# Attention and two gated MLPs on one core: transposed scores of chunks 0 and 1 as 2 x 288 and 2 x 224 columns over two PSUM banks

## The chip, the core and the metric

The program runs on one core of one Trainium2 chip. Its metric is the device time in microseconds, from start to end of one execution; the time of a kernel is the median of several. One execution of the kernel before was also taken by the hardware profiler, which records when each instruction of each engine starts. TensorE is PE in the rows, its weight loads are PEld, VectorE is DVE, ScalarE is ACT, GpSimd is POOL, and SyncE's queue of DMA issues is SPq.

## What is computed

Attention over 4 batches and 8 heads (32 heads in all), 576 positions, head dimension 64, and then two gated MLPs over the 2304 tokens. The attention has a causal mask and a bias that comes from a running sum of `s`:

```python
scores = scale * np.matmul(q, k.transpose(0, 1, 3, 2))
s_pos = np.maximum(s, 0.0)
cum = np.cumsum(s_pos, axis=-1)
bias = -(cum[:, :, :, None] - cum[:, :, None, :])
scores = np.where(causal, -1000000000.0, scores + np.minimum(bias, 0.0))
attn = softmax(scores)                     # exp of scores minus row maximum, over its sum + 1e-9
x = np.matmul(attn, v)                     # heads side by side: 2304 x 512
x = (1 / (1 + np.exp(-(x @ w_gate))) * (x @ w_val)) @ w_out
out = ((x @ w_a) * (x @ w_b)) @ w_out2
```

## The kernel before

**Two parts.** `attention()` runs first, then `mlps()`. Both are written as lists of operations with an engine, dependencies and a priority; `Schedule.emit` puts them in order while the program is built. For attention it is called with `in_order=True` (L718): of the operations that are ready it always takes the one with the smallest priority, and the durations written beside them play no part. The order on each engine is then fixed, and semaphores hold the engines to the data.

**One head.** The 576 keys are cut into five chunks: four of 128 and a tail of 64. `head(i)` (L519) first computes scores with queries on the partitions, for the row maximum (`scores`, L551, into `ps_g`, or `ps_x` for a few; `maxima`, L566, on DVE; a transpose `mT`, L577, into `ps_t`; a copy `mc` on ACT and a DMA `md` that puts the maxima into an extra row of the query operand). Then it computes the scores a second time, transposed, with keys on the partitions: `scores_t(c)` (L588) for each chunk c, over the queries from 128 c to 575 only, since earlier queries may not see these keys. Each such product has a high and a low part, which add up in PSUM: L594 writes, L595 adds.

**Where the transposed scores lie.** The kernel's PSUM tiles have 512 or 1024 fp32 columns, one or two banks, and none of its products crosses from one bank to the next. Chunks 0 and 1 share `ps_e` of two banks (1024 columns): chunk 0, with 576 columns, lies at columns 0 to 575 and is cut at 512, so that one product has 512 columns and one has 64; chunk 1, with 448 columns, lies at 576 to 1023 in one piece. Chunks 2 and 3 (320 and 192 columns) share `ps_f`, and chunk 4 (64) uses `ps_t`. ACT takes the exponential of each of the three tiles in one instruction (`expo`, L597, operations `ex`) and writes it to `pt` in SBUF, with the same order of columns; `P0` (L354) names where each chunk begins in `pt`. POOL then clears the masked half of the diagonal blocks of 128 x 128 (`causal`, L610, operations `cs`): the first two blocks by one instruction, as a list of two blocks at a fixed distance.

**Two heads.** `pair(j)` (L625) takes two heads together. `values` (L635) multiplies `pt` by the values `vx`; the heads lie side by side on PSUM partitions 0 to 63 and 64 to 127 of `ps_x`. It runs once over queries 128 to 575 and once over queries 0 to 127. `sums_of` (L645) multiplies `pt` by ones for the denominators, in five rounds over two thirds of the queries each. These products read `pt` as fp32; the trace records two matmuls for each of them.

**Around it.** In the same loop SP loads q, k and v, POOL and DVE make the low parts (L536, L538), and the first weights of the MLP are loaded and split. DVE, ACT and POOL all take turns between heads. `mlps()` then runs matmuls of 384 and 512 columns on PE (L290 to L292) to the end.

The change touches `P0`, `head` (`cols`, `scores_t`, `expo`, the loop over `ex`, `causal`) and `pair` (`cols_of`, `values`, `sums_of`).

Of the kernel before, what the change touches and what calls it, by code (L numbers as in the profile page):

```python
# [11 lines left out]
ACTF = mybir.ActivationFunctionType  # L12
# [14 lines left out]
class Schedule:  # L27
# [9 lines left out]
    def op(self, name, eng, dur, fn, deps, prio, acq=None, rel=None, lat=None):  # L37
        rel = () if rel is None else rel if isinstance(rel[0], tuple) else (rel,)
        self.ops[name] = (eng, dur, fn, deps, prio, acq, rel, self.LAT if lat is None else lat)
# [80 lines left out]
def attn_mlp_kernel(  # L120
# [14 lines left out]
    nc = tc.nc  # L135


    B, H, S = s.shape
    D = vt.shape[-1]
# [4 lines left out]
    TL = S - 4 * 128  # L144
    rows = [128] * 4 + [TL]
# [9 lines left out]
    scale = 1.0 / float(D) ** 0.5  # L155
# [20 lines left out]
    if wide:  # L176
        u = const.tile([128, 512], I32, name="u")
# [155 lines left out]
    def attention():  # L333
        with ExitStack() as c2:
# [16 lines left out]
            KB = R1 + 2  # L351
            NO, NR2, NX, NPT = 4, 4, 4, 4
            QD, QV = 384, 128
            P0 = [0, 576, 1024, 1344, 1536]  # L354
            CQ1, CK1 = 0, 640
            xt = [tile2([128, S], FP32, f"xt{i}") for i in range(NX)]
            rb = tile2([128, S], FP32, "rb")
# [3 lines left out]
            ones = tile1([128, 32], FP32, "ones")  # L361
# [36 lines left out]
            def more():  # L398
# [4 lines left out]
                for t in pt_t:  # L403
                    nc.vector.memset(t[TL:128, P0[4]:], 0.0)

# [28 lines left out]
            def selectors(o):  # L434
# [3 lines left out]
            sc = Schedule({  # L438
                "g": [psum1("ps_g", 1024)],
                "E": [psum1("ps_e", 1024)],  # L440
                "F": [psum1("ps_f")],
                "t": [psum1("ps_t")],
                "px": [psum1("ps_x", 1024)],
                "raw": list(raw_t),
                "u": [0],
                "W": wslot[:2],
                "stg": stg,
            })
            op = sc.op
# [49 lines left out]
            for i in range(3):  # L499
                op(("relk", i), "SP", 0.65, lambda i=i: nc.sync.dma_start(  # L500
                    out=f32(o_t[i][D:R1, CK1:CK1 + S]), in_=f32(rel[i:NR * BH:BH])), ["sums"] + [("ms", i)] * (i > 0), -210 + i, lat=2.2)
# [17 lines left out]
            def head(i):  # L519
                b, h = divmod(i, H)  # L520
                t0 = HT * i
                o, o2, r, pt = o_t[i % NO], p_t[i % 3], r_t[i % NR2], pt_t[i % NPT]
# [6 lines left out]
                if i >= 3:  # L529
# [7 lines left out]
                    out=k2[up], in0=r[dn], in1=f32(k2[dn]), op=ALU.subtract), [("hk2", i)], (-8.7, -8.3)[i] if i < 2 else t0 - HT - 0.3)  # L537
                op(("loq", i), "DVE" if i < 2 else "Pool", 0.9 if i < 2 else 1.4, lambda: (nc.vector if i < 2 else nc.gpsimd).tensor_tensor(  # L538
                    out=q2[dn], in0=r[up], in1=f32(q1[up]), op=ALU.subtract), [("hq1", i)] + done2, -151 + 2 * i if i < 2 else t0 - HT + 1.45)
# [8 lines left out]
                for g, cs in ((0, (3, 2, 0)), (1, (1, 4))):  # L548
                    to = ("px", ("S", i)) if g and first_at else ("g", (i, g))
# [32 lines left out]
                    out=f32(o[KB:KB + 1, CQ1:CQ1 + 640]), in_=f32(mr)), [("mc", i)] + done, (-8.7, -8.4)[i] + 0.06 if i < 2 else t0 - HT + (3.93, 5.21)[i % 2], lat=2.2)  # L582


                tiles = {0: ("E", (i, 0)), 1: ("E", (i, 0)), 2: ("F", (i, 0)), 3: ("F", (i, 0)), 4: ("t", ("p", i))}
                cols = {0: 0, 1: 576, 2: 0, 3: 320, 4: 0}

                def scores_t(c):  # L588
                    ps = sc.get(*tiles[c])
                    n, c0, q0 = rows[c], cols[c], 128 * c  # L590
                    ks = slice(q0, q0 + n)
                    for a, e in ([(0, 512), (512, 576)] if c == 0 else [(q0, S)]):
                        to = ps[0:n, c0 + a - q0:c0 + e - q0]
                        nc.tensor.matmul(out=to, lhsT=k1[:, ks], rhs=q1[:, a:e], start=True, stop=False)  # L594
                        nc.tensor.matmul(out=to, lhsT=k2[:, ks], rhs=q2[:, a:e], start=False, stop=True)  # L595

                def expo(c0, c1, src):  # L597
                    n = rows[c0]
                    a, e = P0[c0], P0[c1] + S - 128 * c1
                    nc.scalar.activation(  # L600
                        out=pt[0:n, a:e], in_=sc.get(*src)[0:n, cols[c0]:cols[c0] + e - a], func=ACTF.Exp, scale=scale)

                for c in range(NC):
                    op(("ST", i, c), "PE", (0.69, 0.41, 0.3, 0.23, 0.23)[c], lambda c=c: scores_t(c),
                       [("md", i), ("lok", i), ("loq", i)], t0 + (4.2, 4.8, 5.2, 5.5, 5.8)[c], acq=tiles[c] if c in (0, 2, 4) else None)
                for e, (c0, c1, d) in enumerate(((0, 1, 1.05), (2, 3, 0.62), (4, 4, 0.25))):
                    op(("ex", i, e), "ACT", d, lambda c0=c0, c1=c1: expo(c0, c1, tiles[c0]),
                       [("ST", i, c0), ("ST", i, c1), ("pd", (i - NPT) // 2)], t0 + (5.4, HT + 0.3, HT + 0.9)[e], rel=tiles[c0])

                def causal(e):  # L610

                    n, a, st_ = ((128, P0[0], P0[1] - P0[0]), (128, P0[2], P0[3] - P0[2]), (TL, P0[4], 0))[e]
                    w = 2 if st_ else 1
                    to = pt[0:n, a:a + n] if w == 1 else bass.AP(
                        tensor=pt.tensor, offset=pt[0:n, a:a + 1].offset, ap=[list(pt.ap[0]), [st_, 2], [1, n]])
                    nc.gpsimd.affine_select(to, to, [[0, 2], [1, n]][2 - w:], ALU.is_ge, 0.0, base=0, channel_multiplier=-1)
# [8 lines left out]
            def pair(j):  # L625

                t0, b, h = HT * 2 * j, 2 * j // H, 2 * j % H
                vx, x, t = vx_t[j % 2], xt[j % NX], sc_t[j % 2]
                pts = [pt_t[(2 * j + e) % NPT] for e in range(2)]
                pxk = ("px", j) if j < NH // 2 - 1 else ("g", ("pv", j))  # L630

                def cols_of(c, a):
                    return P0[c] + a - 128 * c

                def values(q0, q1_):  # L635
                    px = sc.get(*pxk)
                    js = [c for c in range(NC) if 128 * c < q1_]
                    for c in js:
                        a = max(q0, 128 * c)
                        for e in range(2):  # L640
                            nc.tensor.matmul(  # L641
                                out=px[e * D:(e + 1) * D, QD + a:QD + q1_], lhsT=vx[:, e, c], rhs=pts[e][:, cols_of(c, a):cols_of(c, q1_)],
                                start=c == 0, stop=c == js[-1], skip_group_check=True)

                def sums_of():  # L645

                    px = sc.get(*pxk)
                    rounds = [((0, 0, 192), (0, 384, 576)), ((0, 192, 384), (1, 384, 576)), ((1, 128, 320), (2, 384, 576)),
                              ((2, 256, 384), (3, 384, 576)), ((1, 320, 384), (4, 512, 576))]
                    for n, steps in enumerate(rounds):  # L650
                        for u, (c, a, z) in enumerate(steps):
                            for e in range(2):
                                p = 64 * e + 32 * u
                                nc.tensor.matmul(  # L654
                                    out=px[p:p + 32, a - QD * u:z - QD * u], lhsT=ones, rhs=pts[e][:, cols_of(c, a):cols_of(c, z)],
                                    start=n == 0, stop=n == len(rounds) - 1, skip_group_check=True)

                op(("lv", j), "SP", 1.2, lambda: load_v(j), [("pv", j - 2, 0), ("sel", 1)], t0 + 4.6, lat=3.0)
                op(("pv", j, 1), "PE", 2.6, lambda: values(QV, S), [("cs", 2 * j + e, c) for e in range(2) for c in range(3)] + [("lv", j)], t0 + 3 * HT + 1.3, acq=pxk)
# [34 lines left out]
            for e, (ld, ab, *dv) in enumerate(LOADS):  # L694
                n, m = e // 2, e % 2
                prio = HT * ld + (0.5 if e > 2 else 0)
                last = convert(sc, n, m, [("S", max(int(ld) - 1, 0), 0)], prio,
                               at=[HT * ab + 1.2 - prio] + [HT * dv[k] + 0.95 + y - prio for k, y in ((0, 0), (0, 0.01), (1, 0), (2, 0))])
# [311 lines left out]
```

## Time and profile before

| | |
|---|---|
| median of three runs | 1028.08 us (1027.7 to 1032.49) |
| the profiled execution | 1028.64 us |
| its span, first to last instruction | 1026.9 us |
| mean granted TensorE clock | 0.997 |
| PE busy, share of the span | 98% |
| first matmul of the MLP part | 199.35 us |

Two views count most. The timeline lists instructions in order of time; since matmuls overlap in the records, the cost of one is read from its start to the start of the next, not from its length. The chain of waits follows back from the last instruction what each step waited for; where it names PE, a shorter product can end the program earlier.

### The profile page before, as it was taken

Reading aid. Unit: us, or ns where it says so; the run is one execution under the profiler, and the core shown is the slowest. Engines: PE = TensorE matmul, PEld = TensorE weight load, DVE = VectorE, ACT = ScalarE, POOL = GpSimd, SP = SyncE. Lnnn points to the kernel's source line nnn. Section 1 sums busy time; section 2 is a strip of 40 time slices with the busy share of each in tenths; the row PEclk is TensorE's granted clock in tenths of the full one; section 3 lists DMA queues with packets and bytes.
Section 4 is the critical chain, followed back from the end, with each engine's and each line's share of the span. In section 5 each row is a group of like instructions: output and inputs, shape, how many; then the busy total and the mean of one; then the engine's idle time right before and its main releaser. Section 6 shows DMA issues by size and latency. Waiting matters only on the chain.

```text
span 1026.9 us, 17097 instructions
## 1 busy us (share of the span) xinstructions
PE 1007.2 (98%) x6160; PEld 911.2 (89%) x6160; DVE 691.2 (67%) x1130; ACT 466.3 (45%) x891; POOL 389.3 (38%) x388
## 2 busy tenths in 40 slices
PE   6999999999999999999999999999999999999998
PEld 5777777799999999998888899999999999888886
DVE  7887789889598665779764239867866477932222
ACT  3676767555555454463442245244333334422221
POOL 5578797641555344233200014254533432400000
PEclk8999999999999999999999999999999999999999
DMA  6668786341334223456644342133422245544433
GB/s 171 174 170 203 215 218 188 105 157 47 109 123 144 88 103 112 141 179 205 205 137 123 90 143 72 62 106 125 133 99 103 88 163 175 174 138 133 114 103 102
DMA packets 93586, 139.76 MB, mean 136 GB/s; under 512 B 16215, under 2 KB 54863, under 8 KB 93502
## 3 DMA queue, kind: packets, MB, share of 16 engines
q1 hardware_dynamic: 89234, 133.03, 41.4%
q10 hardware_dynamic: 2988, 4.95, 2.0%
q8 instruction: 48, 0.79, 0.3%
q0 software_dynamic: 1280, 0.70, 0.3%
q14 instruction: 36, 0.29, 0.1%
HBM read 85.53 MB, written 33.45 MB: 116 GB/s over the span
## 4 chain that ended last, share of the span: by engine, by line
PE 82%; DVE 7%; DMA 4%; issue 2%; ACT 1%; POOL 1%; SPq 1%; ACTq 0%; DVEq 0%; POOLq 0%
PE ps L290 24%; PE ps L291 24%; PE ps L292 24%; PE ps_x L641 2%; PE ps_g L557 2%; PE ps_x L654 1%; PE ps_e L594 1%; PE ps_e L595 1%; DVE nm L570 1%; DVE s L823 1%; DMA o<-o 1%; DVE raw L220 1%; DVE u L218 1%; DVE u L216 1%; DMA raw<-in_moe_w_val_dram 1%
## 5 line engine op out<-in xcount | busy, mean ns | idle before, releaser
L290 PE MATMUL ps<-rg,wk 128*128 128x384 f32 (+2 forms) x1128 | 382.1, 339 | 2.5 <-DVE s L823 2.4
L292 PE MATMUL ps<-rg,wk 128*128 128x384 f32 (+2 forms) x1128 | 381.3, 338 | 0.0
L290 PEld LDWEIGHTS ps<-rg,wk 128*128 128x128 f32 x1128 | 211.9, 188 | 8.8 <-DVE s L823 4.5
L292 PEld LDWEIGHTS ps<-rg,wk 128*128 128x128 f32 x1128 | 211.9, 188 | 3.7
L823 DVE TENSOR_TENSOR s<-ps,s 128x384 f32<-128x384 f32 x216 | 119.0, 553 | 114.9 <-PE ps L292 66.5
L291 PE MATMUL ps<-x_sb,wk 128*128 128x384 f32 x576 | 192.6, 334 | 0.0
L836 POOL TENSOR_TENSOR hs<-s,s 128x384 f32<-128x384 f32 x72 | 88.6, 1230 | 265.4 <-issue 93.1
L291 PE MATMUL ps<-rg,wk 128*128 128x384 f32 (+2 forms) x552 | 188.6, 342 | 0.0
L820 ACT COPY s<-ps 128x384 f32<-128x384 f32 x216 | 103.2, 479 | 182.7 <-PE ps L292 180.9
L268 POOL TENSOR_TENSOR wk<-raw,wk 128x512 fp32r<-128x512 f32 x96 | 127.5, 1355 | 147.1 <-ACT wk L265 131.8
L903 DVE TENSOR_TENSOR rg<-rg 128x512 fp32r<-128x512 f32 (+1 forms) x120 | 80.0, 671 | 111.2 <-ACT rg L902 108.4
L902 ACT CAST rg<-rg 128x512 fp32r<-128x512 f32 (+1 forms) x120 | 68.5, 578 | 147.2 <-DMA rg<-hd 109.3
L291 PEld LDWEIGHTS ps<-x_sb,wk 128*128 128x128 f32 x576 | 108.2, 188 | 0.1
L291 PEld LDWEIGHTS ps<-rg,wk 128*128 128x128 f32 x552 | 103.7, 188 | 3.7
L570 DVE TENSOR_REDUCE nm<-ps_g 128x1 f32<-128x512 f32 (+4 forms) x154 | 74.4, 532 | 25.0 <-PE ps_g L562 24.0
L292 PE MATMUL ps<-rg,rg 128*128 128x512 f32 (+1 forms) x228 | 86.2, 378 | 0.0
L290 PE MATMUL ps<-rg,rg 128*128 128x512 f32 (+1 forms) x228 | 86.2, 378 | 0.0
L291 PE MATMUL ps<-rg,rg 128*128 128x512 f32 (+1 forms) x228 | 86.2, 378 | 0.0
L215 ACT ACTIVATE mag<-raw 128x512 f32<-128x512 f32 x72 | 48.3, 671 | 57.1 <-DVE raw L223 31.1
L220 DVE SCALAR_TENSOR_TENSOR raw<-raw,u 128x512 int32<-128x512 int32 x72 | 63.4, 881 | 4.1
L831 ACT ACTIVATE s<-s 128x384 f32<-128x384 f32 x72 | 37.9, 527 | 52.0 <-DVE s L823 51.8
L218 DVE SCALAR_TENSOR_TENSOR u<-raw,u 128x512 int32<-128x512 int32 x72 | 60.4, 839 | 1.5
(119 smaller groups left out, 1495.6 us busy)
## 6 DMA issues: line engine op xcount, KB each, us to landing
hd<-hs SPq DMA_DIRECT2D x72, 384.0 KB
rg<-hd SPq DMA_DIRECT2D x72, 256.0 KB
raw<-in_moe_w_out_dram SPq DMA_DIRECT2D x24, 512.0 KB
r<-in_qk_dram SPq DMA_DIRECT2D x32, 288.0 KB
rg<-hd SPq DMA_DIRECT2D x72, 128.0 KB
raw<-in_moe_w_gate_dram SPq DMA_DIRECT2D x12, 512.0 KB
raw<-in_moe_w_val_dram SPq DMA_DIRECT2D x12, 512.0 KB
raw<-in_moe_w_a_dram SPq DMA_DIRECT2D x12, 512.0 KB
```

The lines of the kernel that those rows point to most:

```text
L218: ("DVE", 0.65, lambda: nc.vector.scalar_tensor_tensor(out=u, in0=parts(n, m)[1], scalar=-0x40000000, in1=u, op0=ALU.bitwise_and, op1=ALU. ...
L220: ("DVE", 0.65, lambda: nc.vector.scalar_tensor_tensor(out=parts(n, m)[1], in0=parts(n, m)[0], scalar=29, in1=u, op0=ALU.logical_shift_rig ...
L268: return lambda: nc.gpsimd.tensor_tensor(out=wcols(n, a, w, 1), in0=src(), in1=f32(wcols(n, a, w, 0)), op=ALU.subtract)
L290: nc.tensor.matmul(out=outp, lhsT=wh, rhs=xh, start=start and e == 0, stop=False, skip_group_check=True)
L291: nc.tensor.matmul(out=outp, lhsT=wh, rhs=xl, start=False, stop=False, skip_group_check=True)
L292: nc.tensor.matmul(out=outp, lhsT=wl, rhs=xh, start=False, stop=stop and e == n - 1, skip_group_check=True)
L570: nc.vector.tensor_reduce(out=nm[0:n, c:c + 1], in_=ps[0:n, p0:p0 + nk], axis=AX.X, op=ALU.max)
L820: op((x,) + key, "ACT", ACT_P, lambda x=x: nc.scalar.copy(out=s(x), in_=bank("X")), [P(p)], end(p) - 10, acq=("s", key + (x,)))
L823: return lambda: nc.vector.tensor_tensor(out=s(x), in0=bank(b_), in1=s(x), op=ALU.add)
L836: op(("h2",) + key, "Pool", PTT, lambda: nc.gpsimd.tensor_tensor(out=half(1), in0=s("s4"), in1=s("s2"), op=ALU.mult), [("c22",) + key, (g[ ...
L902: op(("hh",) + key, "ACT", 0.17 + 0.00083 * N, lambda hs=hs, N=N: nc.scalar.copy(out=hs()[:, 0, 0:N], in_=f32(hs()[:, 1, 0:N])), [("hl",) ...
L903: op(("ho",) + key, "DVE", 0.157 + 0.00104 * N, lambda hs=hs, N=N: nc.vector.tensor_tensor(out=hs()[:, 1, 0:N], in0=f32(hs()[:, 1, 0:N]), ...
```

## The change

The transposed scores of chunks 0 and 1 are cut and placed otherwise in `ps_e` and `pt`. Chunk 1 is cut at query 352 (`QM`) into two products of 224 columns: the first goes to columns 0 to 223, the second to 800 to 1023. Chunk 0 goes between them, at 224 to 799, as two products of 288 columns, whose border at 512 is that of the banks. There are thus eight products a head for these chunks, before six. The exponential covers the same 1024 columns. The mask's two blocks now lie 224 columns apart, before 576. The value and sums products that read chunk 1 on both sides of query 352 read a list of two pieces, and write their output as two pieces that adjoin (new helper `product`). Nothing else differs: operations, priorities, dependencies and tiles are those of before.

```diff
--- before.py
+++ after.py
@@ -351,7 +351,8 @@
             KB = R1 + 2
             NO, NR2, NX, NPT = 4, 4, 4, 4
             QD, QV = 384, 128
-            P0 = [0, 576, 1024, 1344, 1536]
+            P0 = [224, 0, 1024, 1344, 1536]
+            QM = 352
             CQ1, CK1 = 0, 640
             xt = [tile2([128, S], FP32, f"xt{i}") for i in range(NX)]
             rb = tile2([128, S], FP32, "rb")
@@ -583,33 +584,34 @@
 
 
                 tiles = {0: ("E", (i, 0)), 1: ("E", (i, 0)), 2: ("F", (i, 0)), 3: ("F", (i, 0)), 4: ("t", ("p", i))}
-                cols = {0: 0, 1: 576, 2: 0, 3: 320, 4: 0}
+                cols = {0: P0[0], 1: P0[1], 2: 0, 3: 320, 4: 0}
 
                 def scores_t(c):
                     ps = sc.get(*tiles[c])
-                    n, c0, q0 = rows[c], cols[c], 128 * c
+                    n, q0 = rows[c], 128 * c
                     ks = slice(q0, q0 + n)
-                    for a, e in ([(0, 512), (512, 576)] if c == 0 else [(q0, S)]):
-                        to = ps[0:n, c0 + a - q0:c0 + e - q0]
+                    for a, e in ([(0, 288), (288, S)] if c == 0 else [(q0, QM), (QM, S)] if c == 1 else [(q0, S)]):
+                        at = cols[c] + a - q0 + (S if c == 1 and a == QM else 0)
+                        to = ps[0:n, at:at + e - a]
                         nc.tensor.matmul(out=to, lhsT=k1[:, ks], rhs=q1[:, a:e], start=True, stop=False)
                         nc.tensor.matmul(out=to, lhsT=k2[:, ks], rhs=q2[:, a:e], start=False, stop=True)
 
-                def expo(c0, c1, src):
-                    n = rows[c0]
-                    a, e = P0[c0], P0[c1] + S - 128 * c1
+                def expo(c0, n):
+                    p = rows[c0]
+                    a, b_ = (0, 0) if c0 == 0 else (P0[c0], cols[c0])
                     nc.scalar.activation(
-                        out=pt[0:n, a:e], in_=sc.get(*src)[0:n, cols[c0]:cols[c0] + e - a], func=ACTF.Exp, scale=scale)
+                        out=pt[0:p, a:a + n], in_=sc.get(*tiles[c0])[0:p, b_:b_ + n], func=ACTF.Exp, scale=scale)
 
                 for c in range(NC):
                     op(("ST", i, c), "PE", (0.69, 0.41, 0.3, 0.23, 0.23)[c], lambda c=c: scores_t(c),
                        [("md", i), ("lok", i), ("loq", i)], t0 + (4.2, 4.8, 5.2, 5.5, 5.8)[c], acq=tiles[c] if c in (0, 2, 4) else None)
-                for e, (c0, c1, d) in enumerate(((0, 1, 1.05), (2, 3, 0.62), (4, 4, 0.25))):
-                    op(("ex", i, e), "ACT", d, lambda c0=c0, c1=c1: expo(c0, c1, tiles[c0]),
+                for e, (c0, c1, n, d) in enumerate(((0, 1, 1024, 1.05), (2, 3, 512, 0.62), (4, 4, TL, 0.25))):
+                    op(("ex", i, e), "ACT", d, lambda c0=c0, n=n: expo(c0, n),
                        [("ST", i, c0), ("ST", i, c1), ("pd", (i - NPT) // 2)], t0 + (5.4, HT + 0.3, HT + 0.9)[e], rel=tiles[c0])
 
                 def causal(e):
 
-                    n, a, st_ = ((128, P0[0], P0[1] - P0[0]), (128, P0[2], P0[3] - P0[2]), (TL, P0[4], 0))[e]
+                    n, a, st_ = ((128, P0[1], P0[0] - P0[1]), (128, P0[2], P0[3] - P0[2]), (TL, P0[4], 0))[e]
                     w = 2 if st_ else 1
                     to = pt[0:n, a:a + n] if w == 1 else bass.AP(
                         tensor=pt.tensor, offset=pt[0:n, a:a + 1].offset, ap=[list(pt.ap[0]), [st_, 2], [1, n]])
@@ -629,8 +631,13 @@
                 pts = [pt_t[(2 * j + e) % NPT] for e in range(2)]
                 pxk = ("px", j) if j < NH // 2 - 1 else ("g", ("pv", j))
 
-                def cols_of(c, a):
-                    return P0[c] + a - 128 * c
+                def product(out, lhsT, pt, c, a, z, start, stop):
+                    at = P0[c] + a - 128 * c + (S if c == 1 and a >= QM else 0)
+                    rhs = pt[:, at:at + z - a]
+                    if c == 1 and a < QM < z:
+                        rhs = bass.AP(tensor=pt.tensor, offset=pt[:, at:at + 1].offset, ap=[list(pt.ap[0]), [S + QM - a, 2], [1, QM - a]])
+                        out = out.rearrange("p (x n) -> p x n", x=2)
+                    nc.tensor.matmul(out=out, lhsT=lhsT, rhs=rhs, start=start, stop=stop, skip_group_check=True)
 
                 def values(q0, q1_):
                     px = sc.get(*pxk)
@@ -638,9 +645,7 @@
                     for c in js:
                         a = max(q0, 128 * c)
                         for e in range(2):
-                            nc.tensor.matmul(
-                                out=px[e * D:(e + 1) * D, QD + a:QD + q1_], lhsT=vx[:, e, c], rhs=pts[e][:, cols_of(c, a):cols_of(c, q1_)],
-                                start=c == 0, stop=c == js[-1], skip_group_check=True)
+                            product(px[e * D:(e + 1) * D, QD + a:QD + q1_], vx[:, e, c], pts[e], c, a, q1_, c == 0, c == js[-1])
 
                 def sums_of():
 
@@ -651,9 +656,7 @@
                         for u, (c, a, z) in enumerate(steps):
                             for e in range(2):
                                 p = 64 * e + 32 * u
-                                nc.tensor.matmul(
-                                    out=px[p:p + 32, a - QD * u:z - QD * u], lhsT=ones, rhs=pts[e][:, cols_of(c, a):cols_of(c, z)],
-                                    start=n == 0, stop=n == len(rounds) - 1, skip_group_check=True)
+                                product(px[p:p + 32, a - QD * u:z - QD * u], ones, pts[e], c, a, z, n == 0, n == len(rounds) - 1)
 
                 op(("lv", j), "SP", 1.2, lambda: load_v(j), [("pv", j - 2, 0), ("sel", 1)], t0 + 4.6, lat=3.0)
                 op(("pv", j, 1), "PE", 2.6, lambda: values(QV, S), [("cs", 2 * j + e, c) for e in range(2) for c in range(3)] + [("lv", j)], t0 + 3 * HT + 1.3, acq=pxk)
```

## Rows read from the trace of the kernel before

**Rows 1.** The page, part 1: busy microseconds, share of the span, instructions of each engine.
```profile
PE 1007.2 (98%) x6160; PEld 911.2 (89%) x6160; DVE 691.2 (67%) x1130; ACT 466.3 (45%) x891; POOL 389.3 (38%) x388
```

**Rows 2.** Busy time by stretch: stretch, length, busy us (count) per engine, clock, DMA, GB/s.
```profile
125.00:145.00 20.00, 20.00 (x203) 15.37 (x203) 17.81 (x31) 15.61 (x31) 19.48 (x22) 1.00 0.82 225
210.00:400.00 190.00, 189.17 (x1091) 188.85 (x1090) 139.62 (x229) 96.27 (x190) 77.86 (x61) 1.00 0.31 106
```

**Rows 3.** Timeline, PE, a steady head: start us, length us, engine, line, operation, output<-inputs, columns.
```profile
103.09 0.48 PE L594 MATMUL ps_e<-o 128*128 128x512 f32 x1
103.41 0.39 PE L595 MATMUL ps_e<-o 128*128 128x512 f32 x1
103.64 0.19 PE L594 MATMUL ps_e<-o 128*128 128x64 f32 x1
103.67 0.28 PE L595 MATMUL ps_e<-o 128*128 128x64 f32 x1
103.78 0.45 PE L594 MATMUL ps_e<-o 128*128 128x448 f32 x1
104.07 0.36 PE L595 MATMUL ps_e<-o 128*128 128x448 f32 x1
104.26 0.30 PE L594 MATMUL ps_f<-o 128*128 128x320 f32 x1
104.41 0.31 PE L595 MATMUL ps_f<-o 128*128 128x320 f32 x1
104.55 0.25 PE L594 MATMUL ps_f<-o 128*128 128x192 f32 x1
104.64 0.28 PE L595 MATMUL ps_f<-o 128*128 128x192 f32 x1
```

**Rows 4.** Timeline, weight loads (PEld) of the same head.
```profile
103.75 0.19 PEld L594 LDWEIGHTS ps_e<-o 128*128 128x128 f32 x1
103.86 0.19 PEld L595 LDWEIGHTS ps_e<-o 128*128 128x128 f32 x1
```

**Rows 5.** Timeline, PE: first head, its first product and the first of chunk 2.
```profile
18.52 0.79 PE L594 MATMUL ps_e<-o 128*128 128x512 f32 x1
20.71 0.47 PE L594 MATMUL ps_f<-o 128*128 128x320 f32 x1
```

**Rows 6.** Busy time by stretch, PE alone: the granted clock there.
```profile
18.00:20.00 2.00, 1.81 (x8) 0.50 0.97 307
```

**Rows 7.** Chain of waits, start us, length us, what: where it leaves and rejoins PE.
```profile
37.44 0.07 PE ps_t L595
...
62.12 0.28 PE ps_t L577
...
64.77 0.41 PE ps_g L557 x3
...
96.58 0.27 PE ps_t L577
...
140.50 0.22 PE ps_t L577
...
148.38 1.35 DVE nm L570 x3
...
161.24 0.65 PE ps_g L557 x3
```

**Rows 8.** Timeline, PE: scores of the first and last of thirteen heads off the chain.
```profile
40.64 0.48 PE L594 MATMUL ps_e<-o 128*128 128x512 f32 x1
...
158.92 0.47 PE L594 MATMUL ps_e<-o 128*128 128x512 f32 x1
```

**Rows 9.** Chain of waits: sums and values of one pair on PE.
```profile
162.40 1.55 PE ps_x L654 x38
168.10 2.63 PE ps_x L641 x20
```

**Rows 10.** Timeline, PE: the first product of the MLP part.
```profile
199.35 0.44 PE L290 MATMUL ps<-rg,wk 128*128 128x384 f32 x1
```

## The prediction

> **What bounds the kernel now.** I read the page's busy times first: PE is busy for 98% of the span and no other engine for more than two thirds [rows 1]. That is an average, so next come the busy times by stretch. In the MLP part PE is busy 189.17 of 190 us; in the attention part there are stretches where it is busy 20.00 of 20, but POOL is busy 19.48 there and DMA has a share of 0.82 [rows 2]. So PE sets the pace of both parts, and in attention others stand close behind it. The change touches attention alone, after which PE's first MLP product starts at 199.35 us [rows 10].
>
> Third, the timeline of one steady head. The length of a matmul record is no cost here, because records overlap; what counts is the distance from one start to the next. A product of 512 columns is followed 0.23 us later, one of 320 after 0.15 and 0.14, one of 192 after 0.09 [rows 3]. So a column costs about (0.23 - 0.15) / 192 = 0.00042 us. The 64-column products break this: by columns, the pair and the 448-column product behind it should take (64 + 64 + 448) x 0.00042 = 0.24 us, yet from 103.64 to 104.07 the trace shows 0.43 [rows 3]. The loads of weights tell why: they start 0.11 apart there (103.75, 103.86), and the first 448-column product, recorded at 103.78, has its follower only at 104.07, 0.29 later where 0.19 would do [rows 3, 4]. My reading is that a load can begin when the product before it has begun, and that it needs about 0.11 us; a product with fewer columns than that leaves PE waiting for the next weights. So each score product costs the larger of its columns and 0.11.
>
> Fourth, the chain of waits, to see which heads stand on the path. It is on PE for most of attention, but leaves it three times: from 37.5 to 62.12 through ACT, POOL, SP's queue and DMAs, from 65.2 to 96.58 through DMAs and the two queues, and from 140.7 to 161.24 through a DMA and then DVE [rows 7].
>
> **What is removed and added in the scores.** Chunk 0 was products of 512 and 64 columns, chunk 1 one of 448, each with a high and a low part: six products a head. Measured from start to start they take 0.32 + 0.23 + 0.03 + 0.11 + 0.29 + 0.19 = 1.17 us, of which about 0.09 is the first weights' arrival, which stays; 1.08 is left [rows 3]. After: four products of 288 and four of 224. By columns 288 is 0.15 - 32 x 0.00042 = 0.137. For 224 the columns give 0.15 - 96 x 0.00042 = 0.110, and the weights 0.11 [rows 3, 4]: both are as long, so I take 0.11. The sum is 4 x 0.137 + 4 x 0.11 = 0.99. Each head saves 0.09 to 0.10 us of PE, and I take 0.10. Bounds: nothing, if the two added products cost what the short pair lost; and 0.19, if all of the loss of the short pair (0.43 - 0.24) came back.
>
> The first head runs at the 1.2 GHz level (granted clock 0.50 [rows 6]): its six products take 20.71 - 18.52 = 2.19 us [rows 5], 1.87 times those of the steady head, so it saves 0.19. If every head counts, the gain is 31 x 0.10 + 0.19 = 3.3 us.
>
> **Where the gain stays.** I count by the chain. Thirteen heads have their scores while the chain is elsewhere: four from 40.64 on, five between 64.8 and 96.6, and four from 141 to the one at 158.92 [rows 7, 8]. There PE arrives earlier at 62.12, 96.58 and 161.24 and waits longer for ACT, for ACT and for DVE, whose own chains do not hang on these products. The other nineteen keep their gain: 18 x 0.10 + 0.19 = 2.0 us. The MLP part then starts that much earlier, and since PE is all but full there, it passes the gain on to the end.
>
> **What is moved.** The transposed scores of chunks 0 and 1 lie in another order in ps_e and in pt. The exponential still covers 1024 columns in one instruction, and the causal mask still covers two blocks of 128 columns in one instruction; only its stride differs, which I cost at nothing. No DMA, no queue and no wait is moved: the order of issue goes by priorities, and none changes. The exponential is released 0.10 earlier; where ACT is not late already, that helps POOL's mask and costs nothing.
>
> **What the readers of pt get.** Value products of chunk 1 over queries 128 to 575 now read two pieces of 224 columns that start 800 columns apart, and one sums product reads two pieces of 32. No moving operand of the attention products before is in two pieces, so the trace does not show this price. From below it is nothing, since columns and instructions stay the same, and I see no way in which it could gain. From above, as a fixed price, I take the constant of the line through 320 and 512 columns: 0.15 - 320 x 0.00042 = 0.016 us [rows 3]. With two records a product and one such product each in values and in sums, the two heads of a pair side by side, that is 4 x 0.016 = 0.06 a pair, 1.0 us for 16 pairs. I take nothing, because the products of values are paid by the column: 1472 columns a head in 2.63 us [rows 9]. A price by the column is a rival below.
>
> **Sum.** The profiled execution took 1028.64 us, 1026.9 of it the span; less 2.0 it would be 1026.6. It was 0.56 above the median of the three runs, so from the median I forecast 1028.08 - 2.0 = 1026.1 us, a gain of 0.2%. That is less than the 0.5% that a measurement of this kernel can tell from no change.
>
> **Rivals.**
> *All heads count.* The chain is one path of several, and its detours hang on releases by ACT and POOL that might come earlier too. Then the whole 3.3 us shows: 1024.8. For it speaks that PE has whole stretches without a wait [rows 2]; against it, that the chain stays away from PE for 24.6, 31.4 and 20.5 us [rows 7], too long for one late release.
>
> *Others take over.* POOL at 19.48 of 20 and DMA at 0.82 [rows 2] are close behind PE, and a faster PE meets them in the middle of attention also where the chain now lies on PE. Then only the first four heads (0.19 + 3 x 0.10) and six after 161.24 keep their gain, 1.1 us: 1027.0.
>
> *Columns alone count.* If PE were paid by the column, the change would save nothing: 512 + 64 + 448 is 2 x 288 + 2 x 224. Two more products a head at the constant of 0.016 would add 32 x 0.03 = 1.0 us: 1029.1. Against it stand the 0.43 where columns give 0.24 [rows 3]. The Trainium skill has such a rule: "TensorE: Matmul & The Clock Gate", section "Back-to-back issue gap", puts the gap of warm products at columns / 2.4 plus 2.5 ns, with a floor of 25 ns. By that rule alone eight products would take 5 ns a head more than six. The same page's section "LDWEIGHTS (loading the stationary operand)" gives columns / 1.2, 107 ns for 128, and with that the 0.11 of the load rows agrees.
>
> *Two pieces read slowly (slower).* If PE read a moving operand in two pieces at half its rate, chunk 1's value products would cost 448 / 1472 x 2.63 = 0.80 us a pair more, and the sums' 64 columns of 832 in 1.55 us another 0.12 [rows 9]. Sixteen pairs add 14.7 us on PE, and less the 3.3 gained it is 11 us: 1039. It decides for slower than before from the point where these pieces cost over 2 x 0.10 a pair, 22% of the 0.92. For it speaks only that the trace shows no such operand; against it, that nothing about their columns or count changes.
>
> *The short pair's whole loss returns.* At 0.19 a head and all heads counted, 31 x 0.19 + 0.36 = 6.3 us: 1021.8. Against it speaks that 224 columns hardly cover one load.
>
> **How the numbers follow.** Forecast (1026.1) 0.47; all heads 0.22; others take over 0.14; columns alone 0.08; two slow pieces 0.06; whole loss back 0.03. The range from 1024.4 to 1028.6 takes in the first three with 0.4 us of spread below the one, and above the forecast the fixed price of two pieces with the spread of the runs. Faster by over 0.5% is the last case, 0.03; slower by over 0.5% is the slow pieces, 0.06; the rest, 0.91, is within 0.5%.
>
> **What would show it.** In the timeline after, a steady head should go from the first product of 288 to chunk 2's first of 320 in about 1.07 us instead of 1.17: starts 0.13 to 0.14 apart at 288 and 0.11 at 224. Values and sums should stay at 2.63 and 1.55 a pair; if they grow, two pieces have a price. PE's idle time at the three returns of the chain should grow by some 0.4 to 0.5 each; if it does not, all heads count. The first product of the MLP part should start near 197.4 instead of 199.35 us, with no new wait behind it. The prediction is wrong if the 224-column products start more than 0.13 apart, if the values slow down, or if the MLP part gives the gain back.

## The result and the profile after

The kernel after takes 1035.7 us (median of seven executions, 1032.1 to 1037.7) where the kernel before, run beside it, takes 1028.8. The ratio is 1.0054, with a 95% interval of 1.0035 to 1.0074: slower by 5.6 us by that ratio (the two medians differ by 6.9), where 2.0 us less were forecast. The profiled execution of after is the slowest of the seven (1037.73, span 1036.0).

The page of after, part 1 (columns as in [rows 1]): PE's busy time is as before to 1.4 us, although the span is 9.1 longer. PE does not work more, it waits more.

```profile
PE 1005.8 (97%) x6224; PEld 912.9 (88%) x6224; DVE 691.1 (67%) x1130; ACT 466.4 (45%) x891; POOL 388.3 (37%) x388
```

The timeline of a steady head in after, PE and the one DVE row that matters (start, length, engine, line, operation, output<-inputs, columns), which answers to [rows 3]:

```profile
100.07 0.38 PE L596 MATMUL ps_e<-o 128*128 128x288 f32 x1
100.28 0.29 PE L597 MATMUL ps_e<-o 128*128 128x288 f32 x1
100.35 1.35 DVE L571 TENSOR_REDUCE nm<-ps_g 128x1 f32<-128x512 f32 x3 [1.84 <-PE ps_g L563]
100.42 0.29 PE L596 MATMUL ps_e<-o 128*128 128x288 f32 x1
100.55 0.29 PE L597 MATMUL ps_e<-o 128*128 128x288 f32 x1
100.68 0.27 PE L596 MATMUL ps_e<-o 128*128 128x224 f32 x1
100.78 0.27 PE L597 MATMUL ps_e<-o 128*128 128x224 f32 x1
100.90 0.27 PE L596 MATMUL ps_e<-o 128*128 128x224 f32 x1
101.01 0.27 PE L597 MATMUL ps_e<-o 128*128 128x224 f32 x1
101.12 0.32 PE L596 MATMUL ps_f<-o 128*128 128x320 f32 x1
...
101.66 0.22 PE L597 MATMUL ps_t<-o 128*64 128x64 f32 x1
101.75 0.65 PE L558 MATMUL ps_g<-o 128*128 128x256 f32 x3
```

From the first product to chunk 2's first it is 101.12 - 100.07 = 1.05 us, where before took 1.17. After the first one, whose follower comes 0.21 us later, the products of 288 start 0.13 to 0.14 apart, those of 224 0.10 to 0.12. So the local arithmetic holds. Values in two pieces cost nothing either: in the chain of waits of after a pair's values take the same 2.63 us as in [rows 9], and the 42 products of the remaining values and the sums 1.92, as before (0.37 + 1.55).

```profile
174.68 2.63 PE ps_x L640 x20
180.41 1.92 PE ps_x L640 x42
```

And yet the MLP part starts 6.3 us later than in [rows 10] (timeline, PE):

```profile
205.63 0.44 PE L290 MATMUL ps<-rg,wk 128*128 128x384 f32 x1
```

Where in attention? The transposition of a head's maxima on PE (into `ps_t`) marks the heads. From that of head 13 to that of head 17 (the first head is number 0) before takes 22.61 us (first fence), after 25.79 (second):

```profile
84.86 0.27 PE L577 MATMUL ps_t<-idf,nm 128*5 128x128 f32 x1 [0.64 <-DVE nm L570]
107.47 0.27 PE L577 MATMUL ps_t<-idf,nm 128*5 128x128 f32 x1
```

```profile
86.52 0.27 PE L578 MATMUL ps_t<-idf,nm 128*5 128x128 f32 x1
112.31 0.27 PE L578 MATMUL ps_t<-idf,nm 128*5 128x128 f32 x1 [2.10 <-DVE raw L220]
```

The 2.10 in the last row is a wait that the profile puts down to DVE's L220, work on an MLP weight. The chain below leads from there back over DVE to ACT's copy that lands at 103.94 + 5.86 = 109.80 us; how much of this wait belongs to the new order is not separated.

The chain of waits of after in that stretch (start, length, what):

```profile
89.36 6.20 DMA r<-in_qk_dram
...
95.64 0.72 ACTq L582
...
96.40 0.12 ACT o L533
...
99.33 0.28 PE ps_t L578
...
103.94 5.86 DMA o<-o
...
113.30 4.01 DMA o<-o
...
117.33 0.04 ACTq L535
...
117.48 4.86 DMA o<-o
```

L582 is ACT's DMA that puts a head's maxima into the query operand (`o<-mr`). It reads nothing of the load `r<-in_qk_dram`, which fetches another head's queries and keys. Still it is issued at 95.64, 0.08 after that load has landed (89.36 + 6.20 = 95.56), and ACT, which takes its work in order, stands behind it until 96.40. The same holds at 117.33: ACT's copy of the low-part operand of the keys (L535) is issued when SP's copy for the queries has landed. In the chain of before the same instruction, there L581, waits too, but for another stranger, a weight load of the MLP (87.01 + 5.81 = 92.82):

```profile
87.01 5.81 DMA raw<-in_moe_w_val_dram
...
92.84 0.02 ACTq L581
...
92.90 0.72 ACTq L581
```

The reason stands in the two programs' lists of instructions with their waits. On every engine the order of the instructions is the same, apart from the two added products. But SP's and ACT's DMAs share eight completion semaphores (DMAHW0 to DMAHW7), handed out in turn, in the order in which the build's own model of time expects the issues; a DMA also waits for the one that had its semaphore before, eight places ahead. That model charges an fp32 product of fewer than 256 columns four times. It took the kernel for 1032.8 us before and for 1063.3 after, so it interleaved the two queues otherwise. Of the first 330 DMAs, 205 kept the DMA eight places ahead. One of ACT's copies, as both lists have it (before, after; a name such as DMAHW6_49 is a semaphore):

```
177 L534 DMA o_1_218<-o_210 64x576 [waits DVE_49,DMAHW6_49,PE_49,Activation_49]
177 L535 DMA o_1_218<-o_210 64x576 [waits DMAHW3_49,DVE_49,DMAHW7_49,PE_49,Activation_49]
```

The lists also name the stranger of each L582 above. In after's list that issue waits on DMAHW2, whose last holder is the load `r<-in_qk_dram`; in before's list, as L581, it waits on DMAHW1, whose last holder is the load `raw<-in_moe_w_val_dram`. Neither waits on any other DMA.

ACT's waits in after that the profile puts down to a DMA, from 15 to 200 us (engine, line, what for: us in total, times, longest):

```profile
ACT o L533 <- DMA rr_d<-sc: 6.4, 2, 3.3
ACT o L533 <- DMA vx<-in_vt_dram: 2.9, 2, 1.6
ACT pt L602 <- DMA o<-o: 2.7, 2, 1.7
ACT o L533 <- DMA r<-in_qk_dram: 2.7, 2, 1.7
ACT o L533 <- DMA vx<-in_vm_dram: 1.4, 1, 1.4
ACT o L533 <- DMA o<-o: 0.4, 1, 0.4
```

They add up to 16.5 us; the same sum in before is 9.5. (The first line stands for two waits, until 96.40 and until 109.38. The list has L582's issue ahead of both behind a load of `r`, and the chain agrees for the first; the view names another DMA, so the sum is worth more than its lines. Each of the two holds some 0.7 us of the issue itself, and some of the other lines are for data that ACT does read.) PE meets this as waits for ACT's exponentials, which hold `ps_t`: 5.7 us in after, 1.2 in before.

```profile
PE ps_t L578 <- ACT pt L602: 5.7, 5, 2.7
```

Not all of the 6.3 us belongs to the change. The stretch at the 1.2 GHz level fell at 22.5 to 30 us in this execution, where PE had work (first fence: busy time by stretch, PE alone, with columns as in [rows 6]); in [rows 6] it fell earlier. And of the profile's total another 2.3 us are two waits of the MLP part for ACT (second fence: timeline, PE, the wait in brackets), which a second profile of after does not have (after_again: the MLP part begins at 202.59 and takes 827.6 us, as before).

```profile
23.00:30.00 7.00, 5.94 (x24) 0.53 0.79 229
```

```profile
723.20 0.44 PE L290 MATMUL ps<-rg,wk 128*128 128x384 f32 x1 [0.98 <-ACT s L823]
881.87 0.44 PE L290 MATMUL ps<-rg,wk 128*128 128x384 f32 x1 [1.34 <-ACT s L823]
```

### The profile page after: what moved, and what is told of

It is laid out like the page before. It is cut to its first block, busy times and chain, and to the rows that moved or that the text cites. A ratio compares the mean times of both kernels' runs of the same rounds, so it can differ in the third digit from the quotient of the medians.

```text
span 1036.0 us, 17237 instructions
## 1 busy us (share of the span) xinstructions
PE 1005.8 (97%) x6224; PEld 912.9 (88%) x6224; DVE 691.1 (67%) x1130; ACT 466.4 (45%) x891; POOL 388.3 (37%) x388
## 4 chain that ended last, share of the span: by engine, by line
PE 74%; DVE 8%; DMA 6%; issue 2%; ACT 2%; POOL 1%; SPq 0%; ACTq 0%; DVEq 0%; POOLq 0%
PE ps L290 24%; PE ps L291 23%; PE ps L292 23%; DMA o<-o 3%; PE ps_x L640 2%; DVE nm L571 1%; DVE s L826 1%; DMA r<-in_qk_dram 1%; DVE u L218 1%; DMA raw<-in_moe_w_a_dram 1%; PE ps_g L558 1%; DVE raw L220 1%; DVE rg L324 1%; DVE hs L318 1%; DVE x_sb L324 1%
## 5 line engine op out<-in xcount | busy, mean ns | idle before, releaser
L220 DVE SCALAR_TENSOR_TENSOR raw<-raw,u 128x512 int32<-128x512 int32 x72 | 65.7, 912 | 4.1
```

The source lines that it names most:

```text
L220: ("DVE", 0.65, lambda: nc.vector.scalar_tensor_tensor(out=parts(n, m)[1], in0=parts(n, m)[0], scalar=29, in1=u, op0=ALU.logical_shift_rig ...
```

## The experiments

A table of all of them first. "ACT on DMA" is the sum of ACT's waits for DMAs from 15 to 200 us of the profiled execution; "13 to 17" is the distance between the two transpositions, as above. Ratios are to the kernel before, run beside each.

| kernel | median us | ratio, 95% interval | ACT on DMA | 13 to 17 |
|---|---|---|---|---|
| before | 1028.8 | 1 | 9.5 | 22.61 |
| after | 1035.7 | 1.0054 [1.0035, 1.0074] | 16.5 | 25.79 |
| after_again | 1033.5 | 1.0048 [1.0030, 1.0066] | 18.7 | 26.11 |
| map_only | 1033.8 | 1.0046 [1.0026, 1.0065] | 18.4 | 26.09 |
| after_bf16 | 1034.3 | 1.0052 [1.0033, 1.0071] | 14.0 | 25.39 |
| map_back | 1029.1 | 1.0013 [0.9996, 1.0031] | 9.2 | 23.18 |
| map_exact | 1028.6 | 0.9997 [0.9980, 1.0013] | 8.8 | 22.35 |
| other_map | 1029.3 | 1.0004 [0.9988, 1.0021] | 7.1 | 23.81 |
| two_more | 1029.6 | 1.0011 [0.9990, 1.0031] | 7.9 | 23.91 |
| before_bf16 | 1028.9 | 0.9990 [0.9975, 1.0005] | 8.2 | 22.35 |
| less_pe | 1030.3 | 1.0006 [0.9986, 1.0026] | 6.0 | 22.54 |
| before_dve | 1029.8 | 1.0004 [0.9988, 1.0020] | 10.6 | 24.34 |
| less_pe_dve | 1027.6 | 0.9979 [0.9960, 0.9997] | 11.1 | 21.69 |
| before_split | 1035.5 | 1.0053 [1.0032, 1.0074] | 17.6 | 25.68 |
| after_split | 1041.0 | 1.0115 [1.0090, 1.0140] | 35.5 | 26.81 |
| after_more | 1044.5 | 1.0144 [1.0117, 1.0172] | 36.1 | 27.14 |

**Is it the order of the DMAs or PE's work?** The order that counts here is the one in which SP's and ACT's DMAs take the semaphores. It can be turned without turning the work, since the build's model charges bf16 products once, and bf16 products of 224 columns start 0.10 to 0.11 apart as the others do (105.81 and 105.92 in map_back). From a head's first transposed product to chunk 4's first it is 1.56 us in after, in map_back and in map_exact (medians over the 32 heads); before takes 1.66, map_only 1.71, two_more 1.68 and after_bf16 1.45. map_back is after with

```
up = lambda x, wide: x if c != 1 or wide else x.bitcast(BF16)...[:, :, 1]
w = i % 2 == 0 and a == QM
... lhsT=up(k1[:, ks], w), rhs=up(q1[:, a:e], w) ...  up(k2[:, ks], False) ...
```

> The kernel after, but the score products of chunk 1 read only the upper halves of their operands as bf16 (on even heads the first product of the second piece stays whole), so the scores of chunk 1 are rounded; columns, count, banks and pieces are those of after. The build's time model then charges these products once and no longer four times, and its order of DMA issue comes out as in the kernel before: 322 of the first 330 DMAs of SP's and ACT's queues stand behind the same eighth DMA before them, where in after it is 205. Theory 1 (the time went into the changed order of the shared DMA semaphores): the loss is gone and the predicted gain shows, 1026 to 1028 us, first MLP product at 196 to 199 us. Theory 2 (a faster PE in the scores collides with the other engines, or the new columns of ps_e and pt cost something): it stays at 1034 to 1037. Theory 3 (the two added products a head cost): likewise 1034 to 1037.

map_only is before with `[(0, 512), (512, 576)] if c == 0 else [(q0, 352), (352, S)] if c == 1 else [(q0, S)]`, and two_more has `[(0, 256), (256, 512), (512, 576)] if c == 0`:

> The kernel before with its columns and banks, where only chunk 1's product of 448 is cut in place into 224 and 224. The model charges these products four times as in after, and the order of DMA issue is that of after: 326 of the first 330 DMAs stand behind the same eighth DMA. On PE the cut adds 2 x 0.11 - 0.19 = 0.03 us a product, 0.06 a head, 1.9 us for 32 heads. Theory 1 (order of the shared DMA semaphores): the loss of after comes without its gain, 1035 to 1040 us. Theory 2 (collision of a faster PE, or the new columns): no loss but PE's own, 1029 to 1031. Theory 3 (two added products a head cost): 1035 and more, but then also in the control with a third product in chunk 0.

> The kernel before with chunk 0 as 256, 256 and 64 columns in the same places: two more products a head, as in after, and an order of DMA issue that stays near that of before (268 of the first 330 behind the same eighth DMA; the model charges products from 256 columns on once). On PE it adds nothing by columns, at most 2 x (2 x 0.11 - 0.21) = 0.02 a head. Theory 1: 1028 to 1030 us, unless the 62 DMAs that differ cost by themselves. Theory 2: 1028 to 1030. Theory 3 (two added products a head cost): 1034 or more.

> The kernel after once more, for a second profile on the same chip as the other three: 1032 to 1038 us. If the 2.7 us that it lost in the first four heads come from where the stretch of 1.2 GHz falls in that one execution, they are not there in a second; if they come from the order of the semaphores, PE waits again near 24 us and the half clock falls again between 23.6 and 30 us.

With after's work and nearly before's order the loss is gone (1029.1); with before's places and after's order it is there (1033.8, under the 1035 to 1040 expected), of which the cut's own 0.05 us a head can make 1.6 us at most; two added products alone cost nothing that can be told (1029.6). Theories 2 and 3 fall. after_again has its half clock at other places (18 to 22 and 96.5 to 100.5 us) and is back level with before at head 4 (34.94 us; before 34.90, after 37.58), so the early 2.7 us of the first profile of after were that execution's. The 3 us between heads 13 and 17 are there again.

But map_back did not reach the 1026 to 1028 that theory 1 expected of it: the loss went and no gain came. map_exact closes the last difference of order (`w = i in (0, 3, 4, 5, 6, 8, ...) and a == QM`), before_bf16 is the control for the operands (`up` on before's products of 448), other_map has all of chunk 1 in bf16, after_bf16 has chunk 0 in bf16 instead of chunk 1:

> As map_back (the kernel after, chunk 1's score products on the upper halves of their operands, so the scores of chunk 1 are rounded), but the heads whose first product of the second piece stays whole are chosen so that all 632 DMAs of SP's and ACT's queues stand behind the same eighth DMA as in the kernel before. Theory A (the eight DMAs that still differed in map_back took the gain): 1026.0 to 1027. Theory B (others take over: the 0.10 us a head are given back to POOL, DMA and the queues within a few heads): 1028 to 1029.5, as map_back. Theory C (bf16 operands or two pieces cost something): like B, but then the kernel before with bf16 operands is slower than before too.

> The kernel before with nothing but chunk 1's two products of 448 columns reading the upper halves of their operands as bf16 (the scores of chunk 1 are rounded). The order of DMA issue is that of before for all 632. It is the control for map_back and map_exact: theories A and B 1028 to 1029, the time of before; theory C 1029.5 to 1031.

> As map_exact, but all of chunk 1's score products read the upper halves (the scores of chunk 1 are rounded), so PE's work is the same to a hundredth, while the order of DMA issue is a third one: 229 of the first 330 DMAs stand behind the same eighth DMA as in before, 202 as in after. If the order of the shared semaphores sets the time, this run need not agree with map_exact: anything from 1026 to 1036. If only PE's work counts, it is within 1 us of map_exact.

> The kernel after, but chunk 0's score products of 288 columns (not chunk 1's) read the upper halves of their operands as bf16, so the scores of chunk 0 are rounded. The build's time model charges 288 columns the same either way, so the order of DMA issue stays that of after for 330 of the first 330 DMAs. It is the control for map_back and map_exact. Theory 1 (the order of the shared semaphores costs the time): the loss stays, 1032.5 to 1036. Theory C (bf16 operands made map_back and map_exact quick): 1028 to 1030.

map_exact lies between a gain of 2.1 us and a loss of 1.3, so before's order in full brings back before's time and no gain that shows. after_bf16 keeps the whole loss, with 0.11 us a head less on PE than after: bf16 operands do not take the loss away. Chunk 1 in bf16 with after's order was not run; that its products start as far apart as the others, and that map_only loses at full precision, speaks against the operands there. other_map shows that an order that differs from before's as much as after's does need not cost: what counts is which waits it makes.

**What is PE's time in the scores worth?** less_pe is map_exact without the low part of chunk 0 (`if c == 0:` only the product of k1 and q1); other heads' products of chunk 1 stay whole, so that the order of the DMAs stays that of before:

> As map_exact, but the low part of chunk 0's score products is left out: two products of 288 columns a head fewer, 2 x 0.137 = 0.27 us of PE, 8.8 us over 32 heads with the first one at half the clock; 628 of the 632 DMAs stand behind the same eighth DMA as in before, where the order of issue is concerned nothing else differs. It asks what a microsecond of PE's time in the scores is worth. Theory A (PE sets the end in attention): 8 us below map_exact, 1018 to 1020. Theory B (others take over): under half of that, 1024 to 1028.

Taking 0.27 us a head from PE gains nothing that shows: the ratio is 1.0006, the time 1030.3, above even the 1024 to 1028 of theory B. The timeline shows why. Rows of before first, then of less_pe (DVE's maxima of the first group, and PE's next product into `ps_g`, whose buffer these maxima free):

```profile
103.38 1.35 DVE L570 TENSOR_REDUCE nm<-ps_g 128x1 f32<-128x512 f32 x3 [0.98 <-PE ps_g L562]
104.78 0.22 PE L595 MATMUL ps_t<-o 128*64 128x64 f32 x1
104.84 0.63 PE L557 MATMUL ps_g<-o 128*128 128x256 f32 x3
```

```profile
112.18 1.35 DVE L571 TENSOR_REDUCE nm<-ps_g 128x1 f32<-128x512 f32 x3 [1.27 <-PE ps_g L563]
113.22 0.22 PE L603 MATMUL ps_t<-o 128*64 128x64 f32 x1
113.58 0.65 PE L558 MATMUL ps_g<-o 128*128 128x256 f32 x3
```

In less_pe the score products are done early and PE waits until DVE's maxima end: 112.18 + 1.35 = 113.53, and the next product starts 0.05 later. In before DVE ends at 104.73, so by the same 0.05 PE could go on at 104.78; it goes on at 104.84. A head's transposed scores lie beside DVE's maxima, and PE had 0.06 us to gain there, not 0.10. In after it starts 0.05 after DVE's end (100.35 + 1.35 = 101.70, 101.75): the floor is reached. Over a steady pair (transposition of head 29 to that of head 31) it is 10.83 us in before, 10.75 in after and 10.75 in less_pe too; the first two fences are before and after:

```profile
175.72 0.27 PE L577 MATMUL ps_t<-idf,nm 128*5 128x128 f32 x1
...
186.55 0.27 PE L577 MATMUL ps_t<-idf,nm 128*5 128x128 f32 x1
```

```profile
182.26 0.27 PE L578 MATMUL ps_t<-idf,nm 128*5 128x128 f32 x1
...
193.01 0.27 PE L578 MATMUL ps_t<-idf,nm 128*5 128x128 f32 x1
```

If DVE is that floor, a shorter row of maxima must lower it. Both kernels leave out the maximum of query chunk 0 (`if c == 0: continue` in `maxima`):

> The kernel before without DVE's maximum of query chunk 0 (the shortest of the three of the first group, 0.28 us a head; that chunk's column of offsets stays at its first value, so its exponentials are wrong). 628 of the 632 DMAs stand behind the same eighth DMA. Theory F (a head's score products and DVE's maxima run side by side, and the later of the two lets PE go on; in before PE's products are the later one by some 0.04 to 0.1 us): a steady pair of heads stays at 10.8 us, the time at 1027 to 1029. If DVE were already the later one in before, the pair falls to 10.3 and the time to 1021 to 1025.

> The kernel less_pe without DVE's maximum of query chunk 0 as well (so both the low part of chunk 0's scores and that maximum are left out). 624 of the 632 DMAs stand behind the same eighth DMA as in before. Theory F: with less_pe alone a steady pair stood at 10.75 us, DVE's floor; with 0.28 us a head less on DVE it falls to 10.2 to 10.35, and the time to 1021 to 1026, as far as POOL and the DMAs in mid-attention let it. If something else than DVE held the pair at 10.75, it stays there, and the time at 1028 to 1030.

It does. The pair stays at 10.82 us in before_dve, where PE is the later one, and falls to 10.36 in less_pe_dve; the time falls by 0.2% (0.9960 to 0.9997), to 1027.6, which is less than the pairs give and short of the 1021 to 1026 expected; what takes the rest back is not shown. In less_pe_dve PE again goes on right behind DVE (62.82 + 1.16 = 63.98, then 64.03):

```profile
62.82 1.16 DVE L573 TENSOR_REDUCE nm<-ps_g 128x1 f32<-128x512 f32 x2 [0.69 <-PE ps_g L563]
...
64.03 0.65 PE L558 MATMUL ps_g<-o 128*128 128x256 f32 x3
```

**Which of the new waits cost?** In after's list, from ACT's thirteenth DMA on, 18 of its 28 copies of the keys' low-part operand stand eight places behind SP's copy for the queries of the previous head (4 in before, 5 in other_map), and 8 of 29 issues of `o<-mr` behind `sc<-den_d` (2 in before, 4 in other_map). The expectations below count 35 such copies and take the copy for that of the same head; both are wrong, while the 18, 4 and 2 that they name are right. I took these two for the cause. after_split and before_split issue the small load of the row of relations (6.8 KB a head) as two:

```
lambda: [nc.sync.dma_start(out=f32(q1[R1:KB + 1, 0:288]), in_=relq_d[i][:, 0:288]),
         nc.sync.dma_start(out=f32(q1[R1:KB + 1, 288:S]), in_=relq_d[i][:, 288:S])]
```

after_more does the same with SP's copy of q2.

> The kernel after, whole and at full precision, but SP's small load of the row of relations (6.8 KB a head) is issued as two DMAs of half the columns. One more DMA in the ring shifts who stands eight places ahead: of ACT's 35 copies of k2's lower half in the steady heads, 2 then stand behind SP's copy of q2 of the same head (18 in after, 4 in before), and of ACT's 29 issues of o<-mr none behind SP's sc<-den_d (8 in after, 2 in before). Theory 1a (these two kinds of false wait are what costs): the loss goes, 1027 to 1030.5. Theory 1b (it is some other part of the new order, or loads of r and raw ahead of o<-mr, 14 here, 13 in after, 7 in before): 1032 to 1036.

> The control of after_split: the kernel before with the same load split into two. Of the 35 copies 4 stand behind q2's, of the 29 issues 2 behind sc<-den_d and 16 behind a load. Theory 1a: 1028 to 1030. Theory 1b with the loads as the cause: 1031 and more.

> The kernel after with SP's copy of q2 issued as two DMAs of half the columns: 22 of the 35 copies of k2 stand behind one of q2's, 2 of the 29 issues behind sc<-den_d, and 22 behind a load. Theory 1a, if the copies are the larger part: 1032 to 1037, as in after or more. If sc<-den_d is the larger part: 1028 to 1031.

Theory 1a falls: after_split has hardly any of the two and is 5 us slower than after, slower than either theory had it. Loads ahead of `o<-mr` do not sort the kernels either: before has 7 of 29, after 13, after_split 14, before_split 16 and after_more 22, but other_map has 14 and loses nothing. One more DMA a head, with not a byte more to move, costs 0.5%, some 5 us, even in before. One reading is that with one more DMA a head, eight places reach less far back. That is argued: the split also takes SP an issue more a head (0.42 us each in after) and deals out all the semaphores anew, and no run tells these apart. What shows is that ACT waits longer: 35.5 us in after_split and 36.1 in after_more, where PE's waits for ACT's exponentials at `ps_t` grow to 14.9 and 13.8 us. So the table's fourth column, not a count of one kind of link, goes with the time: up to 11.1 us of ACT's waits for DMAs the kernels stand within 0.3% of before, from 14.0 to 18.7 they are 0.5% slower, at 36 over 1%. Which single link costs most stays open. The column is a correlation; the evidence for the order is that the loss goes at after's work (map_back, map_exact) and comes at nearly before's (map_only).

## Why the prediction was wrong

- **"No DMA, no queue and no wait is moved: the order of issue goes by priorities, and none changes."** This step failed, and it alone turned the sign. The order of issue on each engine did stay; the semaphores did not. At equal work on PE the order is worth some 4 to 6 us: the ratios are 0.9997 and 1.0013 in map_exact and map_back, 1.0048 and 1.0054 in after_again and after. No rival named it. The chain of before held the clue: the prediction has it go from 65.2 to 96.58 through DMAs and the two queues, and the rows there (87.01 to 92.90 above) are an issue of `o<-mr` that waits for an MLP weight load.
- **Each head saves 0.10 us of PE.** Right: 1.05 against 1.17 at the places forecast, and 1.56 against 1.66 up to chunk 4's first product. The rival by which columns alone count is refuted: eight products took 0.12 us less than six. The Trainium skill ("TensorE: Matmul & The Clock Gate", section "Back-to-back issue gap") calls the formula that the prediction took from it that of an isolated product, and says that in a stream of weight loads and products both set the spacing. The trace agrees with the latter, by the same 0.12 us.
- **What is read from pt in two pieces costs nothing.** Right: 2.63 us a pair, as before. That rival, the only one priced clearly slower, is refuted; the slow side came by another way.
- **Nineteen heads keep the gain, 2.0 us.** Wrong in size, as far as the pairs tell; map_exact's interval, which reaches down to 2.1 us less, does not exclude it by itself. "PE sets the pace of both parts" was read from PE's busy time [rows 2], but a busy PE was at these products only because they just covered DVE's maxima. By them a steady head could gain (10.83 - 10.75) / 2 = 0.04 us, and 32 such heads 1.3 us, an estimate; map_exact shows nothing that can be told from none. The rival "others take over" was nearest (a gain of 1.1 us), though with POOL and DMA for what was DVE.
- **The first head saves 0.19.** It did not run at 1.2 GHz in the profile of after: its scores (from 18.47 us on) took 1.07 us at the full clock. The half clock came at 22.5 us and met the next head instead, whose scores (from 25.15 on) took 1.93.
- **The MLP part passes the difference on.** Right: it took 827.6 us in after_again as in before.

## What to carry to other kernels

Where a program shares a few completion semaphores among many DMAs, an edit of products alone can change which DMA waits for which: compare the waits in the two lists of instructions, not only the order, and look in the chain for an issue that starts when a transfer lands that it does not read; a small DMA split in two moves no more bytes, and here the kernels with such a split were still some 5 us slower. Before a saving on a busy engine is counted, look up what ends beside it: the gain reaches only as far as the next engine's end, here 0.06 us of 0.10 in a steady head.

## What the runs showed of the hardware

The wait for a semaphore lies ahead of a DMA's row, on the issuing engine: ACT's row of L582 starts at 95.64, 0.08 after the load has landed, and the cast behind it, which has its data, at 96.40. The Trainium skill says the same ("Perfetto Trace Analysis", section "DMA Instruction — HWDGE (DVE, Sync)"): the start that the profile reports is when all semaphores are satisfied. So the time lost to such a wait is idle time ahead of the instructions behind the issue, and the DMA's own row does not show it. It can stand in the row of the semaphore instruction ahead of the issue, but need not: for L582 that row is 0.02 us long at 95.59 and 3.05 us at 105.5, where the issue follows at 108.63.

Stretches at the 1.2 GHz level (granted clock 0.50) lie in the first 40 us, and in some profiles once more near 96 to 121 us, and they differ from execution to execution in number and place: 3.4 us in all in the profiles of before_bf16, less_pe and other_map, 6.8 in before and after, 13.7 in map_exact, 17.1 in before_dve and less_pe_dve (by the profile's own record of the granted clock). One such profile compared with another can be off by several microseconds where PE has work at that time, which is why the table's verdicts go by medians. less_pe, with fewer products, has a mean granted clock of 0.9943 over its twelve executions, and before beside it 0.9968; 0.0025 of 1029 us is 2.6 us, so some of what less_pe spared may have gone there. That is argued, not shown.
